# Loads on either of two queues, zeros first and a new written order: a recurrent attention with a two-layer network behind it, on one Trainium2 core

## The chip, the core and the metric

The kernel runs on one core of one Trainium2 chip. The core has a matrix engine (TensorE, PE in the profile; its weight loads are a row of their own, PEld), three elementwise engines (VectorE or DVE, ScalarE or ACT, GpSimd or POOL) and SyncE (SP), which here only issues transfers. Transfers run on 16 shared DMA engines. SyncE and GpSimd each issue into a queue of their own; each engine works through its instructions in the order in which they were written and waits on semaphores for what another engine or a transfer has to finish.

The metric is device time in microseconds (us) of an execution, the median of several. A profile is one further execution, recorded instruction by instruction; its span runs from the first instruction to the last.

## What is computed

```python
# q, k, v, alpha: (4, 8, 768, 48); w_in: (384, 2048); w_out: (2048, 384), all float32
state = zeros((B, H, D, D))
for t in range(S):
    state = alpha[:, :, t, :, None] * state + einsum('bhd,bhe->bhde', k[:, :, t], v[:, :, t])
    y[:, :, t] = einsum('bhd,bhde->bhe', q[:, :, t], state)
x = y.transpose(0, 2, 1, 3).reshape(B * S, H * D)      # 3072 tokens of 384
out = relu(x @ w_in) ** 2 @ w_out
```

## The kernel before

The 768 steps of each of the 4 sequences are cut into 3 blocks of 256 tokens, which gives 12 units, numbered 0 to 11: first block 0 of every sequence, then block 1, then block 2. Each unit goes through the same stages. In names below, g is the unit.

- *Loads.* Four transfers of 384 KB bring alpha, K, Q and V (`lda`g, `ldk`g, `ldq`g, `ldv`g, L545) into one of four RAW buffers. The two weights come in pieces, cast to bf16 on the way: `win0`, `win1`, `win2` (a quarter, a quarter and a half of w_in) and `wout0`, `wout1` (L513). A table AFTER holds some loads back until an earlier one has landed (`win2` until Q of unit 0, unit 2's loads until `win1`, `wout0` until `win2`, `wout1` until K of unit 2, unit 3's loads until `wout0`); from unit 5 on a load also waits for a step of the unit before.
- *Decays.* Logarithms of alpha (`ln`, from `pr`, the product of two tokens' alpha, for units 2 and up), summed over tokens by matmuls with triangular masks (`m1`), and exponentials of the sums (`ei`, `ea`, `es` on ScalarE); `bk`, `aq`, `lb` make the second token's terms.
- *Keys and queries.* K and Q are scaled (`ekm`, `eqm`) and transposed: on TensorE for units 0 to 2 (`tr`, L609 and L759, with copies `et` out of PSUM), by transposing DMAs from SyncE's queue (L747) for the others. V is cast to bf16 (`vc`, L726 and L727, L591 in unit 0).
- *Attention.* Scores (`p`, L925), a masked copy of them (`mk`, L936), states from K and V (`kv`, L796) with their updates (`sa`, `sc`, `sd`), and the output `y` of a unit (L817 to L864), copied to bf16 (`xe`) and transposed (`xt`; units 0 to 3 on TensorE, with a copy `xv`, the others by DMA, L977).
- *Dense layers.* The first layer has 8 groups of 6 matmuls a unit (`s1_g_u`, L1029), each ended by a maximum with 0 (`re`, on ScalarE L1037 or VectorE L1039); the squares (`sq`) are taken on VectorE (L1047), GpSimd (L1050) or ScalarE (L1051). The second layer has 8 groups of 4 matmuls (`s2_g_j_s`, L1070), copied out (`oe`) and stored (`out`). The last 128 tokens' are cut in two by columns (L997).

Hidden columns 0 to 3 of every 16 (in blocks of 128) need `win0`, 4 to 7 `win1`, the others `win2`; so groups 0 and 1 of a unit need `win0`, 2 and 3 `win1`, 4 to 7 `win2`. Second-layer quarters 0 and 1 need `wout0`, 2 and 3 `wout1`.

What decides the order is a table ORDERS: for each of the five engines the whole sequence of its steps, by name, found by a search ahead of time and written into the source. Steps without a name are numbered by creation (`#11` and `#12` fill two masks, `#21` and `#22` cut them, `#23` copies part of one on ScalarE, `#20` cuts an identity matrix, `#19` fills ZERO). A step stands in the list of the engine that does it, so the table also says which engine does a step that has a choice (`alts`). A planner (`Program.schedule`) runs the sequences against costs in nanoseconds; the kernel takes from it the times by which it leaves out waits that another wait implies. The method `fill` puts matmuls over ZERO into TensorE's idle time ahead of the first dense group, beginning when ZERO is filled by the plan; in ORDERS, ZERO's fill (`#19`) is the last step of VectorE, behind the last copy of the kernel, and no such matmul stands in the built kernel: TensorE's first instruction is that of L567 at 4.93 us.

The start of TensorE's list before, with what bears on the change: `m10_0 m11_0 tr00_0 tr10_0 tr01_0 tr11_0 kv0 p0_0 p1_0 m11 y0 tr0_1 xt0 tr1_1 p0_1 s1_0_2 s1_0_0 s1_0_1 kv1 s1_0_3 y1 s1_0_5 s1_0_4 s1_0_6`. (`m11` without an index behind it is unit 1's `m1`.)

Of the kernel before, what the change touches and what calls it, by code (L numbers as in the profile page):

```python
# [3 lines left out]
ALU = mybir.AluOpType  # L4
# [9 lines left out]
        table ln0_0 ln1_0 ei0_0 #23 ei1_0 ea0_0 ec0_0 ea1_0 vc0 et01_0 ec1_0 ln1 ei1 ea1 xe0 et0_1 ec1 re0_2 re0_0  # L14
        re0_1 sq0_3 re0_5 re0_4 ln2 re0_6 re0_7 es2 ei2 sq0_7 re1_2 ea2 re1_3 sq0_6 re1_5 et1_2 re1_6 sq1_7 sq1_6
        sq1_5 ec2 sq1_1 ln3 oe0_0 ei3 ea3 ec3 es3 vc3 oe1_0 lm4 ln4 ei4 ea4 ec4 oe0_1 es4 re2_0 re2_1 oe1_1 re2_3
        sq2_3 re2_4 ln5 lm5 ei5 ea5 ec5 xe3 re2_7 re2_6 sq2_6 es5 re3_0 re3_1 oe2_0 vc5 re3_3 lm6 xe4 ln6 re3_4 ei6
        oe2_1 re3_7 ea6 ec6 es6 oe3_0 re4_1 re4_0 re4_3 ln7 xe5 ei7 ea7 lm7 ec7 es7 sq4_5 re4_6 re4_7 re5_0 re5_1
# [8 lines left out]
        mk1_0 ekm1 eqm1 xv0 et1_1 sc0 mk1_1 mk0_1 sa1 #2 re0_3 sq0_1 xe1 pr2 xv1 sq0_5 sc1 re1_0 re1_1 bk2 ekm2 eqm2
        re1_4 et0_2 re1_7 mk1_2 mk0_2 sa2 pr3 sc2 bk3 eqm1_3 ekm3 aq3 eqm0_3 pr4 xe2 sa3 xv2 lb4 ekm4 eqm1_4 eqm0_4
        sc3 re2_2 mk1_3 mk0_3 re2_5 sq2_5 sa4 ekm5 xv3 sc4 lb5 eqm1_5 eqm0_5 mk1_4 mk0_4 re3_2 sq3_3 sa5 re3_5 sc5
        sq3_5 bk6 ekm6 re3_6 lb6 eqm1_6 eqm0_6 mk1_5 mk0_5 re4_2 sq4_1 sa6 re4_4 re4_5 sc6 lb7 oe3_1 ekm7 eqm1_7  # L30
        eqm0_7 mk1_6 mk0_6 sd6 re5_3 sa7 sc7 sq5_3 lb8 ekm8 oe4_1 eqm1_8 eqm0_8 mk1_7 mk0_7 sq5_7 sq6_1 re6_2 xe7
# [12 lines left out]
        s2_3_0_3 s1_4_1 s1_4_0 s2_3_1_0 s1_4_3 s2_3_1_1 s1_4_2 y5 s1_4_4 m1i7 s1_4_5 s2_3_1_2 s2_3_1_3 s1_4_7 p0_6
        s1_4_6 s2_4_0_0 s2_4_0_1 s1_5_0 s1_5_1 s2_4_0_2 s1_5_2 s1_5_3 y6 s2_4_0_3 s1_5_4 m1i8 s1_5_5 s2_4_1_0 s2_4_1_1
        s2_4_1_2 s2_4_1_3 s1_5_7 s1_5_6 s2_5_0_0 p0_7 s2_5_0_1 s1_6_0 s1_6_1 s2_5_0_2 s1_6_2 y7 s1_6_3 s2_5_0_3 s1_6_4
        s1_6_5 m1i9 s2_5_1_0 s2_5_1_1 s2_5_1_2 s1_6_7 s1_6_6 s2_5_1_3 p0_8 s1_7_1 s1_7_0 s2_6_0_0 s2_6_0_1 s1_7_3 y8
        s1_7_2 s2_6_0_2 s1_7_5 s2_6_0_3 s1_7_4 m1i10 p0_9 s2_6_1_0 s1_7_7 s2_6_1_1 s1_7_6 s2_6_1_2 s2_6_1_3 s1_8_1
        s1_8_0 s2_7_0_0 s1_8_3 s2_7_0_1 s1_8_2 y9 m1i11 s2_7_0_2 s1_8_4 s2_7_0_3 s1_8_5 s1_8_6 s2_7_1_0 s2_7_1_1
# [1109 lines left out]
```

## Time and profile before

| | |
|---|---|
| Median of 3 runs | 177.78 us (175.22, 177.78, 178.06) |
| Profiled execution, time | 173.93 us |
| Profiled execution, span | 172.2 us |
| Data moved | 33.37 MB in 71,559 packets, 67,568 of them under 512 bytes |
| GpSimd's queue | 8 loads of 384 KB and the 5 pieces of weight |
| SyncE's queue | 40 loads of 384 KB, 18 + 8 transposes, 14 stores |

The profile's first part gives the busy time of each engine and its share of the span. The windows give the same for stretches of the span, in the order PE, PEld, DVE, ACT, POOL, with the number of instructions in brackets, then the granted TensorE clock, the mean share of the DMA engines and GB/s. The chain of waits follows the work that ended last back through what released it. In a timeline each row is one instruction or a merged run of equal ones: start, length, engine, line, operation, output and input; what stands in square brackets is the idle time before it and what ended it. A share of the DMA engines can exceed 1 where packets overlap. Matmuls overlap too: the distance between starts tells their rate, not their length.

### The profile page before, as it was taken

The page shows a single profiled execution, that of the slowest core. Times are in us where ns is not written, and L with a number is a line of the kernel's source. Part 1 is how long each engine was busy: PE and PEld are TensorE (multiplying, and loading weights), DVE is VectorE, ACT ScalarE, POOL GpSimd, SP SyncE. Part 2 cuts the span into 40 slices and gives each one's busy share as a digit, 9 for nine tenths or more (in the row PEclk, how much of TensorE's full clock was granted, in tenths as well). Part 3 has the DMA queues.
Part 4 walks back from the last instruction along what each step waited for, and adds up shares of the span by engine and source line. Part 5 has one row for each costly group of instructions (what it writes and reads, how often), then busy time and mean ns, then how long its engine had stood idle before and what let it go on. Part 6 is the DMA issues. An engine that isn't in the chain of part 4 may idle for free.

```text
span 172.2 us, 5038 instructions
## 1 busy us (share of the span) xinstructions
PE 160.9 (93%) x2200; PEld 127.6 (74%) x2200; DVE 117.2 (68%) x186; ACT 104.5 (61%) x190; POOL 64.6 (37%) x65
## 2 busy tenths in 40 slices
PE   0696999999999999999999999999999999999994
PEld 0564799756788877887877887878777877687773
DVE  4478889768977787769566848799517709355241
ACT  2837478767677866466785578377668454152240
POOL 4947214910286554481640466001012122403700
PEclk9999999999999999999999999999999999999999
DMA  5999999999997999999999999999983672220012
GB/s 139 346 256 244 291 276 212 204 272 297 159 240 183 292 221 179 221 222 251 205 221 293 219 197 243 162 286 317 183 209 115 90 84 93 48 93 0 24 71 91
DMA packets 71559, 33.37 MB, mean 194 GB/s; under 512 B 67568, under 2 KB 68592, under 8 KB 71536
## 3 DMA queue, kind: packets, MB, share of 16 engines
q1 hardware_dynamic: 69024, 26.75, 70.4%
q0 software_dynamic: 2512, 6.29, 15.4%
q8 instruction: 17, 0.28, 0.7%
q14 instruction: 6, 0.05, 0.1%
HBM read 25.17 MB, written 4.72 MB: 174 GB/s over the span
## 4 chain that ended last, share of the span: by engine, by line
PE 90%; DVE 3%; ACT 2%; DMA 2%; issue 1%; DVEq 0%; ACTq 0%
PE psWH L1029 36%; PE psO L1070 33%; PE psX L925 3%; PE psZ L796 2%; PE psX L828 2%; DMA raw<-in_alpha_dram 2%; PE psX L817 2%; PE psWH L1070 2%; PE psX L997 2%; PE psZ L925 1%; PE psWH L669 1%; DVE pm L936 1%; PE psO L1029 1%; PE psX L864 1%; PE psX L971 1%
## 5 line engine op out<-in xcount | busy, mean ns | idle before, releaser
L1029 PE MATMUL psWH<-xt,win 128*128 128x256 bf16 x552 | 71.0, 274 | 0.2 <-ACT rr L1037 0.2
L1070 PE MATMUL psO<-wout,gt 128*128 128x384 bf16 x352 | 66.3, 326 | 0.0
L1029 PEld LDWEIGHTS psWH<-xt,win 128*128 128x128 bf16 x552 | 61.4, 129 | 5.3 <-DVE xt L983 0.6
L1070 PEld LDWEIGHTS psO<-wout,gt 128*128 128x128 bf16 x352 | 33.4, 98 | 17.5 <-DVE gt L1047 0.5
L1037 ACT ACTIVATE rr<-psWH 128x512 bf16<-128x512 f32 x58 | 33.9, 595 | 15.4 <-PE psWH L1029 14.5
L1050 POOL TENSOR_TENSOR gt<-rr 128x1024 bf16<-128x1024 bf16 (+1 forms) x17 | 28.0, 1654 | 37.4 <-ACT rr L1037 20.8
L1039 DVE TENSOR_SCALAR rr<-psWH 128x512 bf16<-128x512 f32 x34 | 23.4, 690 | 19.5 <-PE psWH L1029 19.0
L1051 ACT ACTIVATE gt<-rr 128x512 bf16<-128x512 bf16 (+1 forms) x26 | 21.1, 824 | 5.8 <-DVE rr L1039 5.8
L1077 ACT ACTIVATE osb<-psO 128x384 f32<-128x384 f32 x18 | 8.8, 490 | 17.0 <-PE psO L1070 16.8
L936 DVE TENSOR_TENSOR pm<-psZ,caus 128x1024 bf16<-128x1024 f32 x12 | 14.6, 1220 | 3.1 <-PE psZ L925 3.1
L726 POOL CAST vbf<-raw 128x768 bf16<-128x768 f32 x8 | 6.7, 832 | 24.6 <-DMA raw<-in_v_dram 24.6
L936 DVE TENSOR_TENSOR pm<-psX,caus 128x1024 bf16<-128x1024 f32 x12 | 14.6, 1216 | 0.5 <-PE psZ L925 0.5
L1047 DVE TENSOR_TENSOR gt<-rr 128x1024 bf16<-128x1024 bf16 (+1 forms) x17 | 10.6, 625 | 2.9 <-ACT rr L1037 2.4
L687 POOL TENSOR_TENSOR ek<-ek,raw 128x384 f32<-128x384 f32 x6 | 6.5, 1082 | 15.8 <-ACT ek L680 15.8
L731 DVE TENSOR_TENSOR qks<-raw,eq 128x384 bf16<-128x384 f32 x18 | 9.4, 553 | 2.6 <-DMA raw<-in_q_dram 1.8
L736 DVE TENSOR_TENSOR qks<-raw,ek 128x768 bf16<-128x768 f32 x11 | 10.5, 955 | 0.5 <-POOL ek L687 0.4
L704 DVE TENSOR_TENSOR la<-psWH,la 128x384 f32<-128x384 f32 x8 | 4.4, 553 | 7.9 <-ACT eq L682 6.5
L661 ACT ACTIVATE lab<-prd 128x384 bf16<-128x384 f32 x10 | 5.2, 522 | 4.1 <-POOL prd L660 2.4
L956 ACT ACTIVATE xbf<-psX 128x768 bf16<-128x768 f32 x7 | 5.7, 810 | 3.3 <-PE psX L817 3.0
L660 POOL TENSOR_TENSOR prd<-raw 128x384 f32<-128x384 f32 x5 | 5.2, 1040 | 4.9 <-DMA raw<-in_alpha_dram 4.9
L680 ACT ACTIVATE ek<-psWH 128x384 f32<-128x384 f32 x10 | 4.9, 490 | 3.0 <-PE psWH L672 2.2
L958 DVE CAST xbf<-psX 128x768 bf16<-128x768 f32 x5 | 4.8, 954 | 2.0 <-PE psX L817 1.3
(128 smaller groups left out, 183.7 us busy)
## 6 DMA issues: line engine op xcount, KB each, us to landing
out_dram<-osb SPq DMA_DIRECT2D x11, 384.0 KB, 4.0
raw<-in_alpha_dram SPq DMA_DIRECT2D x10, 384.0 KB, 4.5
raw<-in_k_dram SPq DMA_DIRECT2D x10, 384.0 KB, 4.6
raw<-in_q_dram SPq DMA_DIRECT2D x10, 384.0 KB, 4.8
raw<-in_v_dram SPq DMA_DIRECT2D x10, 384.0 KB, 4.9
wout<-in_moe_w_out_dram POOLq DMA_DIRECT2D x2, 768.0 KB, 8.4
raw<-in_alpha_dram POOLq DMA_DIRECT2D x2, 384.0 KB, 6.5
raw<-in_k_dram POOLq DMA_DIRECT2D x2, 384.0 KB, 7.2
```

Source lines behind the costliest of these rows:

```text
L731: add("dve", lambda e, j=j, dst=dst: e.tensor_tensor(dst, RAW[r][:, 2, :, j, :].rearrange("p (n x) d -> p n x d", x=2), EQ[la][:, j].rearr ...
L736: add("dve", lambda e, a=a, E=E: e.tensor_tensor(QKS[qs][:, a, :, :, 0:D], RAW[r][:, 1 + a].rearrange("p h j d -> p j h d"), E[la][:].rear ...
L925: ins = pe.matmul(psT[64 * c:64 * c + 64, rr_, o:o + 128], keys, mov)
L936: add("dve", lambda e, hf=hf, psT=psT: e.tensor_tensor(PM[pm][:, hf].rearrange("p r n j t -> p (r n) (j t)"), psT[:, :, :].rearrange("p r ...
L1029: ins = pe.matmul(psF[:, i * T:(i + 1) * T], WIN[:, kk, hidden(fj)], mov, start=(kk == 0), stop=(kk == KT - 1))
L1037: add("act", lambda e, psF=psF, rr=rr: e.activation(rr, psF, AF.Relu), act_ns(512), pu + 600, reads=[keyF], writes=[("rr", rb, half)], nam ...
L1039: alts={"dve": (lambda e, psF=psF, rr=rr: e.tensor_scalar(rr, psF, 0.0, None, ALU.max), dve_ns(512))})
L1047: add("dve", lambda e, dst=dst, sq=sq: e.tensor_tensor(dst, sq, sq, ALU.mult), 148 + k * 267, pu + 1200, reads=[("rr", rb, h) for h in ran ...
L1050: alts={"pool": (lambda e, dst=dst, sq=sq: e.tensor_tensor(dst, sq, sq, ALU.mult), 200 + k * 840), "act": (lambda e, dst=dst, sq=sq: e.act ...
L1051: "act": (lambda e, dst=dst, sq=sq: e.activation(dst, sq, AF.Square), act_ns(k * 512))})
L1070: ins = pe.matmul(psS, GT[gt][:, fj, j, :], WOUT[:, fj, :], start=(fj == 0), stop=(fj == FT - 1))
L1077: add("act", lambda e, j=j, psS=psS: e.activation(OSB[ob][:, j], psS, AF.Copy), act_ns(DM), ps_ + 700, reads=[keyS], writes=[("osb", ob, j ...
```

## The change

The five sequences are replaced by newly searched ones. With them:

- Loads of units 1 to 11 may stand in SyncE's list or in GpSimd's (EITHER, `alts`). Eight move to GpSimd: K of 3, V of 4, K of 5, V of 7, alpha and K of 9, alpha and V of 11. V of unit 1 moves from GpSimd to SyncE. Unit 2's K is issued ahead of its Q, unit 1's Q ahead of its K.
- ZERO's fill (`#19`) is VectorE's first step. The method `fill` is gone; 21 matmuls over zeros stand in TensorE's list by name, 16 of 512 columns and 5 of 256: seven ahead of the first `m1`, the others in between up to the first dense group.
- ScalarE's `#23` stands ahead of the first logarithm. V of unit 0 is cast on GpSimd. `s1_0_2`, the first dense group, stands ahead of `p0_1`, the scores of unit 1.
- Of the steps that have a choice, 104 change between the elementwise engines: 36 from VectorE to ScalarE, 34 from ScalarE to VectorE, 10 from GpSimd to VectorE, 9 from GpSimd to ScalarE, 8 from ScalarE to GpSimd, 7 from VectorE to GpSimd.
- The planner's costs change: how GpSimd and VectorE hold each other up, a slow TensorE before 9,000 ns, the cost of a change of matmul shape, and some fixed durations.

```diff
-        m10_0 m11_0 tr00_0 tr10_0 tr01_0 tr11_0 kv0 p0_0 p1_0 m11 y0 tr0_1 xt0 tr1_1 p0_1 s1_0_2 s1_0_0 s1_0_1 kv1
-        s1_0_3 y1 s1_0_5 s1_0_4 s1_0_6 xt1 s1_0_7 m1s2 m1i2 s1_1_0 s1_1_1 s1_1_2 s1_1_3 s1_1_4 s1_1_5 s1_1_6 tr0_2
-        tr1_2 s1_1_7 s2_0_0_0 p0_2 s2_0_1_0 s2_0_1_1 s2_0_0_1 kv2 s2_0_0_2 s2_0_0_3 s2_0_1_2 m1i3 s2_0_1_3 s2_1_0_0
...
+        fill512_0 fill512_1 fill512_2 fill512_3 fill512_4 fill512_5 fill256_6 m10_0 m11_0 fill512_7 tr00_0 fill512_8
+        fill512_9 fill512_10 tr10_0 tr01_0 tr11_0 kv0 p0_0 p1_0 fill512_11 fill256_12 m11 fill512_13 fill512_14
+        fill512_15 fill512_16 fill256_17 y0 tr0_1 fill512_18 fill256_19 xt0 tr1_1 fill256_20 s1_0_2 p0_1 s1_0_0 s1_0_1
+        kv1 s1_0_3 y1 s1_0_4 s1_0_6 xt1 s1_0_7 m1i2 s1_0_5 m1s2 s1_1_2 s1_1_1 s1_1_0 s1_1_5 tr0_2 s1_1_3 s1_1_4 tr1_2
+        s1_1_6 s2_0_0_0 p0_2 s2_0_0_1 s1_1_7 s2_0_0_2 s2_0_0_3 s2_0_1_0 kv2 s2_0_1_1 m1i3 s2_1_0_0 s2_1_0_1 s2_1_0_2
...
     "pool": """
-        #22 #15 #21 #14 #20 lda1 ldk1 ldq1 win1 win0 ldv1 win2 lda2 ldq2 ldk2 ldv2 vc1 wout0 wout1 aq2 sq1_3 sd1 sd0
-        vc2 sd2 bk4 sq2_1 pr5 vc4 sd3 bk5 sq2_7 sq3_1 sd4 pr6 sq3_7 sq3_6 vc6 sd5 pr7 sq4_3 bk7 vc7 pr8 sq5_1 bk8 vc8
-        pr9 sq6_3 bk9 sq6_6 sq6_5 vc10 bk11 vc11 sq9_3 sq9_7 sq10_1 sq10_6 sq11_1 sq11_3
+        #21 #22 #14 #15 lda1 #20 ldq1 ldk1 win1 vc0 win0 win2 lda2 ldk2 vc1 ldq2 sd0 ldv2 wout0 wout1 sq0_6 aq2 sq1_3
+        ldk3 vc2 sq1_7 ldv4 pr4 bk4 ldk5 sd3 pr5 sq2_3 bk5 sd4 vc5 pr6 sq3_3 bk6 vc6 sd5 sq4_3 ldv7 bk7 sq4_6 pr8
+        sq5_3 lda9 ldk9 vc8 bk9 sq6_3 sq6_6 sq6_5 lda11 sq7_7 pr11 sq8_3 ldv11 vc11 sq9_7 sq9_6 sq10_1 sq10_3
     """,
     "sp": """
-        lda0 ldk0 ldq0 ldv0 lda3 ldq3 ldk3 ldv3 lda4 ldk4 ldv4 ldq4 tr0_3 tr1_3 lda5 ldk5 tr0_4 tr1_4 out0_1 ldq5 ldv5
...
+        lda0 ldk0 ldq0 ldv0 ldv1 lda3 ldq3 ldv3 lda4 ldq4 ldk4 tr0_3 tr1_3 lda5 out0_1 tr0_4 tr1_4 ldq5 ldv5 out1_1
...
+    EITHER = tuple(range(1, G))
...
-            load_op[name] = add(ring, lambda e, dst=dst, src=src: e.dma_start(dst, src), cost, at,
-                writes=[key], name=f"ld{name}", dma=f"{nm}{r}{ring}", lag=1230 if ring == "sp" else 1180,
+            go = lambda e, dst=dst, src=src: e.dma_start(dst, src)
+            load_op[name] = add(ring, go, cost, at,
+                writes=[key], name=f"ld{name}", dma=f"{nm}{r}", lag=1230 if ring == "sp" else 1180,
+                alts={"sp": (go, 600), "pool": (go, 930)} if g in EITHER else None,
...
+    for name in ORDERS["pe"].split():
+        if name.startswith("fill"):
+            n = int(name[4:7])
+            add("pe", lambda pe, n=n: pe.matmul(psO[:, 0:n], ZERO[:, 0:128], ZERO[:, 0:n], skip_group_check=True),
+                216 if n == 512 else 109, 0, reads=[("zero",)], name=name)
     pr.schedule()
-    pr.fill(lambda n: lambda pe: pe.matmul(psO[:, 0:n], ZERO[:, 0:128], ZERO[:, 0:n], skip_group_check=True),
-            ((512, 216, 420), (256, 109, 250)), min(o.start for o in pr.order["pe"] if o.name.startswith("s1_")), zero, 4600)
```

More of the change, by code (lines that the diff above doesn't have):

```diff
@@ L13 @@
     "act": """
[L14 to L18, printed above, removed]
@@ L27 @@
[L27 to L31, printed above, removed]
@@ L44 @@
[L44 to L48, printed above, removed]
```

119 lines of the change are left out of this document (56 added, 63 removed).

## The prediction

> **What bounds the kernel now.** I read the page first, then the busy time by stage, then the chain of waits of the first 21 us, then the timelines of the queues that load. The span and the busy shares:
>
> ```profile
> span 172.2 us, 5038 instructions
> PE 160.9 (93%) x2200; PEld 127.6 (74%) x2200; DVE 117.2 (68%) x186; ACT 104.5 (61%) x190; POOL 64.6 (37%) x65
> ```
>
> The view of busy time by windows cuts the span in three (PE, PEld, DVE, ACT, POOL busy, clock, DMA share, GB/s):
>
> ```profile
> 1.00:18.20 17.20, 9.73 (x187) 7.50 (x188) 11.63 (x30) 9.73 (x18) 11.64 (x17) 1.00 1.06 259
> 18.20:170.00 151.80, 151.21 (x2018) 120.14 (x2014) 105.03 (x155) 94.60 (x172) 52.71 (x45) 1.00 0.86 189
> 170.00:172.20 2.20, 0.00 (x0) 0.00 (x0) 0.45 (x2) 0.00 (x0) 0.00 (x0) 1.00 0.28 89
> ```
>
> From 18.2 to 170 TensorE is idle for 0.6 us in all. A new order can win next to nothing there; it can only lose. What can be won lies ahead of 18.2, where TensorE is idle for 7.5 us. There the chain of waits reads (start, length):
>
> ```profile
> 6.36 0.30 ACT caus L485
> 9.26 1.03 PE psZ L609 x8
> 10.29 0.76 PE psWH L796 x16
> 11.04 0.60 PE psX L925 x16
> 12.81 1.23 DVE pm L936
> 16.40 0.56 DVE xt L983
> 16.96 0.61 DVE kqt L766
> 17.61 0.42 PE psX L925 x16
> 18.25 0.78 PE psO L1029 x6
> 20.34 0.45 PE psZ L796 x16
> ```
>
> L1029 at 18.25 is the first dense group; everything dense waits for it. Two things are to be seen. A mask for later use (6.36) stands between two exponentials that the chain needs. And the dense group stands behind the scores of unit 1 (17.61), which wait for a copy that it doesn't need: its own input is copied by 16.96.
>
> The early matmuls are also slow. TensorE's timeline shows the same work twice:
>
> ```profile
> 9.26 1.03 PE L609 MATMUL psZ<-ident,qks 128*128 128x128 bf16 x8 [0.42 <-DVE kqt L616]
> 11.98 0.45 PE L633 MATMUL psWH<-laf,linc 128*128 128x384 bf16 x1
> 12.26 0.33 PE L634 MATMUL psWH<-laf,linc 128*128 128x384 bf16 x1
> 12.42 0.33 PE L635 MATMUL psWH<-laf,linc 128*128 128x384 bf16 x1
> 14.99 0.62 PE L759 MATMUL psZ<-ident,qks 128*128 128x128 bf16 x8
> ```
>
> Eight transposes take 1.03 at 9.26 and 0.62 at 14.99; the 384-column matmuls follow each other after 0.28 at 11.98 and 0.16 at 12.26. So TensorE ran at about half rate until 12.2, though the page's clock row stands at 9 throughout and doesn't show it.
>
> The transfers set a second bound. GpSimd's and SyncE's timelines, with what ended each wait, the first uses on TensorE, and the DMA by stage:
>
> ```profile
> 4.56 1.09 POOL L545 DMA_DIRECT2D raw<-in_alpha_dram  x1 [0.35 <-DMA raw<-in_alpha_dram]
> 13.90 0.93 POOL L545 DMA_DIRECT2D raw<-in_alpha_dram  x1 [3.36 <-DMA win<-in_moe_w_in_dram]
> 17.63 0.82 POOL L726 CAST vbf<-raw 128x768 bf16<-128x768 f32 x1 [0.17 <-DMA raw<-in_v_dram]
> 21.44 0.71 POOL L513 DMA_DIRECT2D wout<-in_moe_w_out_dram  x1 [2.98 <-DMA win<-in_moe_w_in_dram]
> 25.69 0.58 POOL L513 DMA_DIRECT2D wout<-in_moe_w_out_dram  x1 [3.55 <-DMA raw<-in_k_dram]
> 22.30 0.87 PE L1029 MATMUL psO<-xt,win 128*128 128x256 bf16 x6
> 35.72 1.48 PE L1070 MATMUL psO<-wout,gt 128*128 128x384 bf16 x8
> 4.00:20.00 16.00, 11.54 (x203) 9.30 (x204) 11.30 (x18) 9.52 (x19) 10.57 (x13) 1.00 1.13 277
> 28.00:34.00 6.00, 6.00 (x86) 5.16 (x85) 4.90 (x7) 5.05 (x10) 4.53 (x4) 1.00 0.92 195
> wout<-in_moe_w_out_dram POOLq DMA_DIRECT2D x2, 768.0 KB, 8.4
> ```
>
> The last third of the first weight (win2) is there at 21.44 and first used at 22.30, 0.9 later. The second half of the other (wout1) is issued at 25.69, lands 8.4 later at 34.1 and is first used at 35.72, 1.6 later. The DMA share is over 1 up to 20 and 0.92 from 28 to 34: these landings go by bytes, and TensorE is only 0.9 and 1.6 us behind them.
>
> **The change, part by part.** The sum is made against the profiled execution, 173.93 (span 172.2 and 1.73 around it).
>
> *Start.* The mask goes ahead of the first logarithm, while ScalarE waits for data: -0.30. Zeros are filled first, and 21 matmuls over zeros (16 of 512 columns, 5 of 256) keep TensorE busy from about 1.3. If that brings full rate, the slow pieces of the chain shrink to their later sizes: transposes 1.03 to 0.62, states 0.76 to 0.45, scores 0.60 to 0.42, together -0.90. The price of the zeros: 512 columns are an estimate of 0.37 each at the slow spacing and 0.21 at the fast one; seven run before TensorE has anything to do, the other fourteen are 2.5 to 4.4 us in an idle time of some 3.5, so they could delay it by 1. V of unit 0 is cast on GpSimd instead of ScalarE: 4.56 + 1.09, a selection, two loads, a weight's issue and the cast end near 9.3, and the states are due at 10.29 - 0.30 - 0.41 = 9.6, so it costs nothing. Dense group 2 goes ahead of the scores of unit 1: 18.25 becomes 16.96 plus a little, -1.2. Together the first dense group starts near 15.8 instead of 18.2, -2.4.
>
> *What the transfers leave of it.* In the new order the first group that needs win2 comes after unit 1's output. The same work took 4.7 before (17.61 to 22.30); from 15.8 on that is 20.5, and the masks, whose scores now start a group later, make it some 21.0. win2 is there at about 21.4: -0.8 against 22.30. wout1 waits for K of unit 2, which moves from third to second of its unit, one issue of 0.89 earlier; I take wout1 0.7 earlier, at 33.4. The new order needs it sooner: it puts two second-layer groups and a state (1.4, as eight such matmuls at 35.72 take 1.48 with their tail, and 0.45 at 20.34; 1.9 in all) behind that point, which is 33.9 at the old pace. So 33.9 - 33.4 leaves -0.5. The ends: wout1 no earlier, +0.2; TensorE's own pace, -0.8. The zeros' possible 1 us is covered by the 1.9 that the transfers take back.
>
> V of unit 1 moves to SyncE's queue. The DMA queues differ in their packets (packets, MB, share of 16 engines):
>
> ```profile
> q1 hardware_dynamic: 69024, 26.75, 70.4%
> q0 software_dynamic: 2512, 6.29, 15.4%
> ```
>
> Share times span times 16 over the count gives 28 ns for a packet of SyncE's queue (q1) and 169 ns for one of GpSimd's (q0). If the engines serve the two in turn, V's 64 packets on each engine (1,024 runs of 384 bytes over 16) wait for one of GpSimd's each: 64 x 197 ns from about 7 ends near 20, where it was 17.6 (the cast at 17.63). Cast, state, output and the next dense group then follow near 23.1, 0.8 behind the old 22.30. That is the start's bad end, +0.8; bytes alone bring V no later than now, and I take that, since GpSimd itself stands waiting for win1 until 13.90 in that time and its queue runs thin.
>
> *The steady part.* Eight loads move from SyncE to GpSimd and one the other way:
>
> ```profile
> 34.00:132.00 98.00, 97.60 (x1388) 76.59 (x1386) 73.98 (x110) 67.75 (x126) 35.98 (x32) 1.00 1.05 225
> L545 POOL DMA_DIRECT2D raw<-in_k_dram x2 | 1.8, 890 | 0.0
> POOL vbf L726 <- DMA raw<-in_v_dram: 24.6, 6, 8.7
> POOL prd L660 <- DMA raw<-in_alpha_dram: 4.9, 5, 1.6
> ```
>
> Each holds GpSimd 0.89, net 6.2 us. GpSimd is busy 36 of the 98 us from 34 to 132, and that idle time hides them. SyncE's queue, with the transposes behind those loads, is relieved, but TensorE waits for none of them now. ScalarE's, VectorE's and GpSimd's elementwise steps are dealt out anew, with about the same sums. The ends are -0.6 (the idle time above) and +6.2 (each load felt whole); I take +0.1, beside the lower end, because of the 62 idle us.
>
> [...]
>
> *The end.* VectorE's 0.45 after 170 holds the zeros' fill, which moves to the start; the last stores run beside it: 0. The planner's changed costs emit no instruction: 0.
>
> Sum: 173.93 - 0.5 + 0.1 = 173.5, for an execution like the profiled one.
>
> **From there to the median.** The runs shown go from 175.22 to 178.06 with the median at 177.78, so 3.85 over the profiled execution. Something early can differ that much. From 18.2 on TensorE never rests, so each us at half rate costs 0.5. If half rate lasted beyond 12.2, unit 0's output, the transposes, the second scores would cost an estimated 1.0 more (by 0.41 for eight transposes, 0.18 for scores), and 2.85 more would take 5.7 us of dense work at half rate, until near 25. I take this for the likelier cause, since the trace shows TensorE leaving half rate only after 3 us of nearly unbroken work (9.26 to 12.2), and the next unbroken stretch begins at 17.6. The new kernel is busy with zeros from 1.3 and nearly without a gap from 4.9, so each execution should come to full rate before 12, and the median falls to the sum: 173.5.
>
> [...]
>
> **The rivals.**
>
> *The spread stays.* If the 3.85 come from transfers (the DMA share is over 1 up to 20), or the zeros don't bring full rate sooner, the new kernel keeps that distance: 177.78 - 0.4 = 177.4, no change. For it: the early landings go by bytes. Against: the waits for them are short in TensorE's time, 0.9 and 1.6 us of margin. A part of the spread removed gives 174.3 to 177.
>
> *GpSimd's queue becomes the bound.* It works in order, and a load at its head waits for its buffer and for the load before it. The two rows of waits show it standing for V up to 8.7 at once and 4.1 on average (24.6 by 6), for alpha 1.0 (4.9 by 5). Today a cast or product follows such a wait; in the new order squares for the second layer follow moved loads too, and TensorE takes a late square as a stall. If each of the seven loads is felt with its 0.89 and 0.3 to 1.0 of wait, the sum grows by 8 to 13: 182 to 187, I name 182.5, slower. It decides from 1.1 us per load over the likeliest case, or 0.6 if the spread stays. Against: 62 us of idle time.
>
> **The numbers.** A measurement of this kernel tells about 2% from no change: 174.2 and 181.3 are the bounds. The forecast has 0.46, nearly all of it under 174.2; the spread staying, wholly or partly, 0.34; GpSimd's queue as the bound 0.20. So faster 0.46, within 2% 0.34, slower 0.20. The likeliest case alone reaches from 172.6 (-0.8 and -0.6 in place of -0.5 and +0.1) to 174.7 (+0.8 in place of -0.5, about 1.2 higher). The range goes on to the spread's 177.4 and one us more for the start's bad end on top of it: 172.0 to 178.5, which leaves the slower case out.
>
> **What would show it.** Right: the first dense group (L1029) near 16, ahead of the scores; matmuls of 384 columns 0.16 apart before 12; the wait of the first wout1 group short, or none; TensorE idle under 1 us from 34 to 170; runs close to each other. Wrong: transposes at 9 still near 1.03; V of unit 1 landing after 19; stalls in the middle whose releaser is a square or cast on GpSimd, or a moved load; or a spread as wide as before.

## The result, and the profile after

| | time (us) | ratio to before, 95% interval |
|---|---|---|
| Before, in the same measurement | 176.5 (174.72 to 178.06) | |
| After | 184.18 (182.49 to 184.99) | 1.051 [1.0405, 1.0616] |
| After, a second measurement | 181.44 (178.27 to 183.05) | 1.0278 [1.0131, 1.0426] |
| After, a third, on another chip | 179.33 (177.88 to 182.09, and one of 420.26) | 1.0229 [1.0174, 1.0284] |

The change makes the kernel slower, by 2 to 5 points, where 173.5 and a gain had been forecast. A ratio compares only fast executions, those within 1.5% of the fastest of their kernel, while medians and ranges take in all. (The execution of 420.26 us comes back in the last section.) The profiled execution of after took 184.99, the longest of the first measurement's four. Its page begins with the span and the busy shares, and the fourth part gives the shares of the chain that ended last; the last row is that part before:

```profile
span 183.2 us, 5075 instructions
...
PE 164.7 (90%) x2219; PEld 127.2 (69%) x2221; DVE 120.0 (65%) x187; ACT 107.8 (59%) x193; POOL 65.8 (36%) x68
...
PE 50%; DMA 38%; DVE 5%; POOL 3%; issue 2%; ACT 2%; POOLq 0%; DVEq 0%
...
PE 90%; DVE 3%; ACT 2%; DMA 2%; issue 1%; DVEq 0%; ACTq 0%
```

No engine's busy time grew by more than 3.8 us, the span by 11.0, and transfers hold 38% of the chain where they held 2%. The view of waits, TensorE alone, from 18 us on (total, times, longest), says where TensorE stood:

```profile
PE psWH L1009 <- DMA xt<-xbf: 3.8, 3, 1.5
PE psWH L649 <- ACT lab L641: 2.8, 2, 1.9
PE psX L905 <- DMA kqt<-qks: 1.9, 1, 1.9
PE psO L1050 <- DVE osb L1059: 1.6, 1, 1.6
PE psO L1050 <- DMA wout<-in_moe_w_out_dram: 0.5, 1, 0.5
PE psX L837 <- DVE smd L874: 0.3, 1, 0.3
```

10.9 us in all, against 0.4 in the same view before; 10.5 of the 11.0 are these waits. The dense layer (L1009) waits for transposing DMAs of the output; the first sums of decays (L649) for a cast of ScalarE whose input alpha came late; the scores (L905) for transposed keys; a second-layer group (L1050) for a copy by VectorE that stands in the list behind two products of Q, which wait for a load.

The worst place is unit 4's two transposes. SyncE's timeline, the issues between 49 and 50 with their microseconds to landing, and the windows (PE, PEld, DVE, ACT, POOL, clock, DMA share, GB/s):

```profile
49.35 3.80 SPq L727 DMA_TRANSPOSE kqt<-qks  x2
59.79 0.37 SPq L523 DMA_DIRECT2D raw<-in_q_dram  x1
```

```profile
raw<-in_k_dram POOLq DMA_DIRECT2D x1, 384.0 KB, 10.0
kqt<-qks SPq DMA_TRANSPOSE x1, 10.4
```

```profile
53.00:55.00 2.00, 2.00 (x69) 1.88 (x69) 1.25 (x3) 1.75 (x4) 1.60 (x1) 1.00 1.33 117
55.00:57.00 2.00, 2.00 (x20) 1.57 (x18) 1.74 (x4) 1.83 (x5) 1.68 (x2) 1.00 1.09 84
57.00:59.00 2.00, 1.67 (x15) 1.31 (x12) 0.00 (x0) 1.61 (x4) 0.11 (x1) 1.00 0.98 91
```

K of unit 5, now on GpSimd's queue, is in flight beside them; all three take some 10 us (the second transpose 9.8), and the DMA engines, busy throughout, move 84 to 117 GB/s. Q of unit 5, behind the transposes on SyncE's queue, is issued only at 59.79. That made the moved loads my first suspect. The second profile of the same kernel (178.27) doesn't show it:

```profile
span 176.5 us, 5075 instructions
```

```profile
PE psWH L1009 <- DMA xt<-xbf: 2.7, 2, 1.6
PE psWH L649 <- ACT lab L641: 1.3, 1, 1.3
PE psWH L1009 <- ACT osb L1057: 0.6, 1, 0.6
PE psX L837 <- DVE smd L874: 0.3, 1, 0.3
```

Unit 4's transposes land in 6.3 and 5.5 there; 4.9 us of waits are left, 4.5 over before's 0.4, and the span is 4.3 longer. So the loss is TensorE's waiting, some 4.5 us of it in a good execution and 10.5 in a bad one. Most of the 4.9 belongs to three output transposes, and unit 5's shows how. Its issue, its microseconds to landing and its first use, before and in the second profile:

```profile
76.08 2.02 SPq L977 DMA_TRANSPOSE xt<-xbf  x1
xt<-xbf SPq DMA_TRANSPOSE x1, 4.5
81.68 1.47 PE L1029 MATMUL psWH<-xt,win 128*128 128x256 bf16 x12
...
76.97 1.94 SPq L957 DMA_TRANSPOSE xt<-xbf  x1
xt<-xbf SPq DMA_TRANSPOSE x1, 6.3
83.40 1.47 PE L1009 MATMUL psWH<-xt,win 128*128 128x256 bf16 x12 [1.62 <-DMA xt<-xbf]
```

Before, it landed at 80.56 and was used 1.12 later. The output transposes of units 4 to 8 landed 0.47 to 1.87 ahead of their first use there, those of units 9 to 11 2.85 to 3.98 ahead. In the changed order TensorE comes for those of units 5, 6 and 8 4.5 to 4.8 after their issue, where it came 5.1 to 6.3 after, and they take 5.0 to 6.3, where they took 4.5. It stands 1.62, 0.64 and 1.12 for them. (The view puts the 0.64 down to a copy; that transpose landed 0.14 ahead of the group's start, as the other two did.)

At the start, the first dense group:

```profile
17.26 0.84 PE L1009 MATMUL psO<-xt,win 128*128 128x256 bf16 x6
```

It came at 18.19 before, and at 16.74 in the second profile.

### The profile page after: what moved, and what is told of

The parts are those of the page before. It is cut to its first block, busy times and chain, and to the rows that moved or that the text cites. A ratio compares the mean times of both kernels' runs of the same rounds, so it can differ in the third digit from the quotient of the medians.

```text
span 183.2 us, 5075 instructions
## 1 busy us (share of the span) xinstructions
PE 164.7 (90%) x2219; PEld 127.2 (69%) x2221; DVE 120.0 (65%) x187; ACT 107.8 (59%) x193; POOL 65.8 (36%) x68
## 4 chain that ended last, share of the span: by engine, by line
PE 50%; DMA 38%; DVE 5%; POOL 3%; issue 2%; ACT 2%; POOLq 0%; DVEq 0%
PE psO L1050 22%; PE psWH L1009 18%; DMA kqt<-qks 9%; DMA xt<-xbf 6%; DMA wout<-in_moe_w_out_dram 5%; DMA raw<-in_q_dram 5%; DMA raw<-in_k_dram 4%; DMA win<-in_moe_w_in_dram 4%; DMA raw<-in_alpha_dram 3%; POOL raw L523 2%; PE psX L808 2%; PE psWH L1050 2%; PE psZ L776 2%; PE psX L977 1%; PE psX L797 1%
## 5 line engine op out<-in xcount | busy, mean ns | idle before, releaser
L1009 PE MATMUL psWH<-xt,win 128*128 128x256 bf16 x552 | 70.1, 273 | 3.9 <-DMA xt<-xbf 3.8
L1050 PE MATMUL psO<-wout,gt 128*128 128x384 bf16 x352 | 66.7, 326 | 2.1 <-DVE osb L1059 1.6
L1009 PEld LDWEIGHTS psWH<-xt,win 128*128 128x128 bf16 x552 | 61.7, 129 | 9.7 <-ACT osb L1057 3.0
L1017 ACT ACTIVATE rr<-psWH 128x512 bf16<-128x512 f32 x67 | 39.3, 595 | 39.0 <-PE psWH L1009 38.3
L1050 PEld LDWEIGHTS psO<-wout,gt 128*128 128x128 bf16 x352 | 32.8, 98 | 19.8 <-DVE osb L1059 1.9
L1019 DVE TENSOR_SCALAR rr<-psWH 128x512 bf16<-128x512 f32 x25 | 17.2, 687 | 8.0 <-PE psWH L1009 7.7
L1031 ACT ACTIVATE gt<-rr 128x1024 bf16<-128x1024 bf16 (+1 forms) x24 | 21.1, 893 | 1.3 <-DVE rr L1019 1.1
L1027 DVE TENSOR_TENSOR gt<-rr 128x1024 bf16<-128x1024 bf16 (+1 forms) x19 | 13.1, 693 | 6.2 <-ACT rr L1017 6.2
L716 DVE TENSOR_TENSOR qks<-raw,ek 128x768 bf16<-128x768 f32 x11 | 10.5, 954 | 5.1 <-DMA raw<-in_k_dram 5.0
L706 POOL CAST vbf<-raw 128x768 bf16<-128x768 f32 x6 | 5.0, 830 | 18.9 <-DMA raw<-in_v_dram 18.9
L1057 ACT ACTIVATE osb<-psO 128x384 f32<-128x384 f32 x13 | 6.4, 491 | 6.4 <-PE psO L1050 6.3
L523 POOL DMA_DIRECT2D raw<-in_alpha_dram x4 | 3.8, 959 | 16.6 <-ACT rr L1017 8.0
L871 DVE TENSOR_TENSOR smd<-psZ,sbd 128x384 bf16<-128x384 f32 x8 | 4.4, 554 | 7.3 <-PE psX L797 7.3
L1059 DVE COPY osb<-psO 128x384 f32<-128x384 f32 x9 | 5.0, 557 | 6.1 <-PE psO L1050 6.1
L938 DVE CAST xbf<-psX 128x768 bf16<-128x768 f32 x7 | 6.7, 953 | 3.3 <-PE psX L797 2.2
```

The costliest lines, as they stand in the source:

```text
L523: go = lambda e, dst=dst, src=src: e.dma_start(dst, src)
L716: add("dve", lambda e, a=a, E=E: e.tensor_tensor(QKS[qs][:, a, :, :, 0:D], RAW[r][:, 1 + a].rearrange("p h j d -> p j h d"), E[la][:].rear ...
L938: alts={"dve": (lambda e: e.tensor_copy(XBF[x2][:], psX[:, :, 0:HD]), dve_ns(2 * HD))})
L1009: ins = pe.matmul(psF[:, i * T:(i + 1) * T], WIN[:, kk, hidden(fj)], mov, start=(kk == 0), stop=(kk == KT - 1))
L1017: add("act", lambda e, psF=psF, rr=rr: e.activation(rr, psF, AF.Relu), act_ns(512), pu + 600, reads=[keyF], writes=[("rr", rb, half)], nam ...
L1019: alts={"dve": (lambda e, psF=psF, rr=rr: e.tensor_scalar(rr, psF, 0.0, None, ALU.max), dve_ns(512))})
```

## The experiments

In the names of experiments, "back" is the changed program with the eight moved loads on SyncE's queue again. Ratios are to the kernel before on the same chip, whose median lay between 174.79 and 176.13 there. The theories have letters; A to D stand in the first expectations, E to I come with the results. One thing holds for all runs called "the kernel before with" something, but the one with thin stores alone: they are the changed program with the old lists put in, so the planner's changed costs, and with them the choice of the waits that are left out, are in them too. The three with least else changed (one load moved, and zeros at the start) come out at 1.0038 to 1.0051, so these costs are worth about half a point at most, unless those edits won back what the costs lost.

### Is it the moved loads?

```diff
 pool: -ldk3 -ldv4 -ldk5 -ldv7 -lda9 -ldk9 -lda11 -ldv11
 sp:   ... ldq3 +ldk3 ldv3 lda4 ldq4 ldk4 +ldv4 tr0_3 tr1_3 lda5 +ldk5 out0_1 tr0_4 ... xt5 +ldv7 ...
```

> The changed kernel with all eight loads issued by SyncE again, everything else as changed. Theory A (loads from GpSimd's queue and SyncE's transposing DMAs in flight together hold each other up): the transposes of unit 4, 10.4 us in the changed kernel, land in 4 to 6.5; the three stalls of TensorE that follow them (1.9, 1.6, 1.9 us) and the 1.5 us before unit 7's dense groups go; time 176 to 178.5 against 184.2. Theory B (the new dealing of the elementwise steps is what is late, wherever the loads are issued): 182.5 to 185.

180.67 us, 1.0313 [1.0241, 1.0386]; stalls of 7.6 us. Unit 4's transposes took 5.9 and 4.0 and TensorE didn't wait for them, as theory A had it, but the time lies between both theories' ranges: most of the waiting has another cause. Next, the one suspect alone (K of unit 5 back on SyncE's queue), and the same load alone moved in the kernel before:

> The changed kernel with one load, K of unit 5, issued by SyncE again. Theory A: unit 4's transposes land in 4 to 6.5 us instead of 10.4, and the stalls of 1.9, 1.6 and 1.9 us go with this one load: 178 to 180.5. Theory B: within 1 us of the changed kernel, 183 to 185.

181.68 us, 1.0269 [1.0159, 1.0379], between the theories again and with a wide spread (178.01 to 185.97).

> The kernel before with one load moved, K of unit 5 to GpSimd's queue behind unit 4's second-token product, so that it is issued about when unit 4's transposes are. Theory A: that load and the two transposes land after 8 to 10.5 us instead of 4.6 and 4.0 to 6.2, TensorE waits for unit 4's scores, and the time grows by 2 to 5 us over the kernel before. Theory B: the load lands in 5 to 7 us and the time stays within 1 us.

177.1 us, 1.0051 [1.0018, 1.0083]; the load was issued at 46.68, ahead of the transposes, and landed in 5.4, they in 6.9 and 5.5: theory B's numbers. So it was put later, behind them:

```diff
 pool: ... bk4 sq2_1 +ldk5 pr5 ...
```

> The kernel before with K of unit 5 moved to GpSimd's queue as in the last such run, but three steps later in its list, so that it is issued at about 49.6 us, after the two transposes of unit 4 (from 47.4 us) and not before them as then (46.7 us). Theory A (a load on GpSimd's queue that is issued while SyncE's transposes are in flight holds these up): the transposes land 9 to 10 us after their issue instead of 6.2 and 6.9, the load in some 10, and the ratio is 1.01 to 1.02. Rival (the 10 us in the changed kernel came from something else that lay there, the store issued at 48.1 or unit 4's other loads): 6 to 7 us, ratio 1.005 or less.

175.91 us, 1.0038 [0.9987, 1.0089]. The load was issued at 50.74, two us behind the transposes (48.70), as in the changed kernel's bad place; it landed in 6.0 and they in 5.4 and 6.2, near the rival's numbers. All eight in the kernel before:

```diff
 pool: ... sd1 +ldk3 ... vc2 +ldv4 ... bk4 +ldk5 ... sq4_3 +ldv7 ... sq5_1 +lda9 bk8 +ldk9 ... sq6_5 +lda11 ... bk11 +ldv11 ...
```

> The kernel before with the eight loads moved to GpSimd's queue at about the times at which they were issued, all other orders as before. The forecast's step on the steady part (eight loads cost 0.89 us each on an engine that idles): 1.00 to 1.005. Theory A (each such load that is in flight beside SyncE's transposes holds them up): 1.015 to 1.03, with transposes or loads that land 8 to 10 us after their issue.

179.29 us, 1.024 [1.0157, 1.0324]. The ratio is theory A's, but not its long landings: behind 30 us none took 8, and unit 4's transposes took 7.0 and 6.6. Its two large stalls, 1.91 and 1.57 us, come by GpSimd. The first: VectorE's two products of Q before, then in this run, with GpSimd's square and the second of the two masked copies behind the products, for which TensorE waited until 63.53:

```profile
57.88 1.03 DVE L731 TENSOR_TENSOR qks<-raw,eq 128x384 bf16<-128x384 f32 x2 [0.87 <-DMA raw<-in_q_dram]
...
58.48 2.73 DVE L715 TENSOR_TENSOR qks<-raw,eq 128x384 bf16<-128x384 f32 x2 [1.43 <-DMA raw<-in_q_dram]
58.88 1.91 POOL L1034 TENSOR_TENSOR gt<-rr 128x1024 bf16<-128x1024 bf16 x1 [2.13 <-ACT rr L1021]
62.27 1.21 DVE L920 TENSOR_TENSOR pm<-psX,caus 128x1024 bf16<-128x1024 f32 x1
```

Q came 0.6 later, so the second product started at 58.96, just behind the start of GpSimd's square, and ended at 61.21, 0.4 behind its end: it took 2.25 instead of 0.55. Before, the second was under way when the square began (58.84) and ended at 58.91. The second stall comes from where I had put a load in GpSimd's list (start, length, idle time before and its end):

```profile
92.58 0.93 POOL L527 DMA_DIRECT2D raw<-in_alpha_dram  x1 [3.35 <-ACT rr L1021]
93.53 1.02 POOL L671 TENSOR_TENSOR ek<-ek,raw 128x384 f32<-128x384 f32 x1
```

The load stands at the head of the list for 3.35 us, and the product behind it, which VectorE needs, starts at 93.53, where the kernel before had it at 88.34. In the changed kernel that product (`bk8`) is VectorE's, so nothing of the kind follows this load there.

Then the direct comparison, both kernels on one chip:

> The changed kernel, measured beside the next one on one chip. Theory A (the moved loads cost about 2 of the 5 points): 1.04 to 1.05, 1 to 2 points above the next kernel. Theory I (the loss is the new orders' alone; where the loads are issued decides only which transfer is late): within half a point of the next kernel, both at 1.025 to 1.045.

> The changed program with the eight loads on SyncE's queue, measured beside the kernel above. Theory A: 1.02 to 1.03. Theory I: the same as the kernel above to half a point.

After 179.33 us, 1.0229 [1.0174, 1.0284]; loads back 179.86 us, 1.0306 [1.0241, 1.037]. The moved loads cost nothing in the new orders on this chip; the 0.8 of a point by which the kernel with them is ahead isn't clear of the intervals. Theory A falls as the cause of the loss here. Theory I holds in kind; its half a point was missed by a little. The first measurement's 1.051 was never set beside the loads back on one chip, so what its 2 to 3 points more are isn't shown, and the 10 us landing remains a fact of one profile.

### Is it the new start?

The zeros and ZERO's early fill, put into the kernel before:

> The kernel before with ZERO filled first and the 21 matmuls over zeros in TensorE's list, nothing else moved. Theory C (the spread of the kernel before comes from when TensorE leaves half rate): full rate by the first sums at 5 us, runs within 1.2 us of each other, median 173 to 174.5. Theory D (the spread comes from transfers): full rate by 5 us as well, but runs that spread by 2 to 4 us as before and a median of 175.5 to 177.5.

177.5 us, 1.0043 [0.9993, 1.0094], 174.49 to 182.43. Full rate by 5 us, which both theories had taken for granted, wasn't there in the profiled execution: its 192-column matmuls at 4.9 follow each other after 0.14 to 0.16, much as before (0.13 to 0.16), where the changed kernel's first profile has 0.08. The spread didn't shrink, so theory C falls, and 0.75 us gained at unit 2's state (34.52 for 35.27) were gone at the end.

### Is it single places in the new orders?

The program with the loads back waits in the dense layer for three output transposes, once for a copy and once for a cast. Where such a transposing DMA stands in SyncE's list (its rows in the loads-back program, and the transfer's landing):

```profile
76.41 1.17 SPq L528 DMA_DIRECT2D raw<-in_k_dram  x1
78.40 0.37 SPq L528 DMA_DIRECT2D raw<-in_q_dram  x1
78.81 1.45 SPq L962 DMA_TRANSPOSE xt<-xbf  x1
```

```profile
xt<-xbf SPq DMA_TRANSPOSE x1, 5.1
```

Its input was ready at 77.23 (76.29 and 0.94 for the cast). It was issued 1.58 later, behind Q, and landed 5.1 after that.

```diff
 sp: ... +xt5 ldk7 ldq7 -xt5 ... +xt6 ldk8 ldq8 -xt6 ... +xt8 ldv10 ldq10 out5_1 -xt8 ...
```

> The changed program with all eight loads on SyncE's queue, and in SyncE's list the transposes of the output of units 5, 6 and 8 put ahead of the two loads, of K and Q of a later unit (8: of V, Q and a store), that stood before them. Theory E (what is left of the loss after the loads are back is cover that the new order took from three kinds of transfers and steps: the output's transposes are issued behind loads, land 5 to 6 us later instead of 3.5 to 4.5, and the dense layer waits for them): the three stalls of 1.36, 1.35 and 0.97 us go, the span falls from 179.2 by 3 to 3.7 us, the ratio from 1.031 to about 1.01. Theory F (the landing is slow because the cast ahead of it now lies on VectorE, or because of whatever else is in flight, not because of the place in the list): the transposes land as late as before and the ratio stays at 1.03.

182.56 us, 1.0422 [1.0328, 1.0517]. The three transposes landed in 2.8 each where they had taken 5.1, 6.1 and 5.7, and the waits for them are gone. Other waits took their place, 7.8 us in all for 7.6:

```profile
PE psWH L1014 <- DVE rr L1024: 4.5, 3, 2.5
PE psX L910 <- DMA kqt<-qks: 1.9, 1, 1.9
PE psWH L654 <- ACT lab L646: 1.0, 2, 0.7
```

VectorE's timeline shows what its maximum (L1024), for which TensorE now waits, had to stand behind:

```profile
84.54 0.96 DVE L721 TENSOR_TENSOR qks<-raw,ek 128x768 bf16<-128x768 f32 x1 [3.16 <-DMA raw<-in_k_dram]
85.42 0.68 DVE L1024 TENSOR_SCALAR rr<-psWH 128x512 bf16<-128x512 f32 x1
...
98.93 0.56 DVE L716 TENSOR_TENSOR qks<-raw,eq 128x384 bf16<-128x384 f32 x1 [4.42 <-DMA raw<-in_q_dram]
99.41 0.68 DVE L1024 TENSOR_SCALAR rr<-psWH 128x512 bf16<-128x512 f32 x1
```

The loads that were passed came late, and everything behind them on VectorE with them. Theory E is right about why a transpose lands late, and wrong in taking that for the cost: what one transfer gains the next one loses. The 2.9 us by which the span grew, 182.1 for 179.2, are another matter. Unit 6's scores already start 2.1 later (82.09 for 79.98), ahead of the first moved transpose's use: TensorE had stood 1.92 for unit 4's keys, which the move doesn't touch, and its granted clock had fallen to half behind that wait (0.50 from 60 to 62). It fell once more behind the wait of 2.46 that came with the move (0.52 from 102 to 104; last section).

```diff
 dve: ... sq2_6 +oe2_0 eqm0_5 eqm1_5 -oe2_0 ...
 pe:  ... s1_3_4 -m1i6 s2_2_1_2 y4 s2_2_1_3 +m1i6 ...
```

> The changed program with all eight loads on SyncE's queue, and two steps moved: the eviction of unit 2's first dense output ahead of unit 5's two Q products on VectorE (which wait for a load), and unit 6's first cumulative matmul two matmul groups and one output step later on TensorE. Theory E: the stalls of 1.2 us (dense output on its eviction) and 0.8 us (that matmul on ScalarE's cast) go, about 2 us of the span, the ratio from 1.031 to about 1.02. Rival (the wait only moves on, since the loads of units 5 and 6 are late whatever waits for them): the stalls come back within 3 us at the Q products, the scores of unit 5 or the dense layer, and the ratio stays at 1.03.

181.6 us, 1.0375 [1.0297, 1.0453]: both stalls went. A wait of 1.97 came at unit 4's scores, with a fall of the clock behind it (0.50 from 60 to 62), but that is ahead of both moved steps; behind them the dense layer waited 1.07 for ScalarE. The rival's ratio came, then, without its mechanism being shown. From unit 6's scores to the end this execution takes 97.0 us, and two profiles of the same program without the two moves (loads back, on two chips) take 99.3 and 97.3: one profile can't settle 2 us here.

> Both of these edits together in the changed program with its loads on SyncE's queue. Theory E: 5 to 5.7 us off the span of 179.2, ratio 1.00, and TensorE's idle time after 34 us under 2.5 us. The rival of a loss that moves on: 1.015 to 1.03.

183.45 us, 1.0476 [1.0394, 1.0559], above both ranges. 8.0 us of waits are left, the longest, 2.55, for VectorE's maximum, again with a fall of the clock behind it (0.55 from 100 to 102). Places cured singly gave nothing back.

### Is it SyncE's list, or the compute lists?

> The changed program with its loads on SyncE's queue, and with SyncE's whole list taken from the kernel before (V of unit 1 is the one load that has no place there and goes behind unit 0's); the lists of the four compute engines are the changed ones. Theory H (the order on SyncE's queue is at fault: transfers stand there in an order that lands the wrong ones late): the span falls to 172 to 175 us, ratio 1.00 to 1.01. Theory G (the DMA engines are a second bound, busy for 97 to 117% of every 10 us from 10 to 120 us in the kernel before, so that no order lands the loads sooner, and the changed compute orders ask for some units about three matmul groups earlier than they can come): stalls of 5 to 8 us stay, at other places, ratio 1.03 to 1.04.

181.5 us, 1.0215 [1.0096, 1.0334], between the two; the stalls stay (6.9 us), as theory G said, at other places: one transpose now takes 6.8 and holds the dense layer for 2.48.

> The kernel before with SyncE's list in the changed order (all loads on SyncE's queue, but V of unit 1, which stays on GpSimd's as before). Theory H: 1.02 to 1.03. Theory G, with the compute orders at fault: 1.00 to 1.01.

178.62 us, 1.0159 [1.0055, 1.0262]. Both halves cost: SyncE's new list alone 1.6 points with the old compute lists, and the new compute lists some 2 points even with SyncE's old list. Both intervals exclude no change and are about 2 points wide. Neither H nor G as put holds the whole.

### Is it the time of the transfers?

The stores of units 0 to 10 cut to an eighth:

```diff
-    e.dma_start(dst, OSB[ob][:].rearrange("p j n -> p (j n)"))
+    e.dma_start(dst[:, :96], OSB[ob][:].rearrange("p j n -> p (j n)")[:, :96])
```

> The changed kernel whole, but for the stores of units 0 to 10, which write an eighth of their bytes (96 of 768 numbers of a row): some 11% less to move, all orders and queues as they are, the output incomplete. Theory G (what the changed orders lose is lost to transfers that the DMA engines have no time for): the stalls at transposes and loads shrink to 1 to 4 us and the ratio to 1.00 to 1.02. Rival (the stalls come from the order of waits among engines whatever the DMA engines have to move): 1.04 to 1.05 as in the whole kernel.

176.3 us, 1.0022 [0.9971, 1.0073]: theory G's ratio. The whole kernel wasn't run on this chip, but this interval lies below all three of the whole kernel. What is left of the stalls isn't known: the profiled execution took 182.65, far from that median, and stood 7.9 us. The control:

> The kernel before with the stores of units 0 to 10 cut to an eighth of their bytes, as in the changed kernel's thin run. Theory G (in the old order the transfers just keep up, and TensorE, idle for 0.6 us, is the bound): 0.990 to 1.000, so that the 5 points which the thin stores gave the changed kernel are its own. Rival (the thin stores help any order alike): 0.95 to 0.97.

174.86 us, 0.9992 [0.9952, 1.0032]: the old order gains nothing from 11% less to move, so what the thin stores gave the changed kernel, 2 to 5 points by the measurement, is its own.

> The changed program with all loads on SyncE's queue (ratio 1.031 in full) and the thin stores. Theory G: 0.99 to 1.005, stalls of TensorE after 18 us of 2 us in all or less. Rival (the new compute orders wait in their own lists): 1.015 to 1.03.

177.47 us, 1.0134 [1.0033, 1.0235], between the two: by the middle values more than half of 1.0306 is gone; 4.6 us of stalls are left.

```profile
PE psWH L1014 <- DMA xt<-xbf: 2.6, 3, 1.1
PE psWH L654 <- ACT lab L646: 1.4, 2, 0.8
PE psX L910 <- DMA kqt<-qks: 0.6, 1, 0.6
```

> The kernel before with the eight loads on GpSimd's queue (ratio 1.024 in full) and the thin stores. Theory G (all of the loss is transfers' time): 0.99 to 1.005. Rival (a part is GpSimd's own list: an issue of 0.93 us ahead of a product that VectorE waits for, as at 92.6 us in the full run, where TensorE then stood 1.57 us): 1.008 to 1.015.

180.48 us, 1.0302 [1.0186, 1.0417]: no help here, and above both ranges. The load at the head of GpSimd's list held it for 4.32 us at the same place, and TensorE stood 2.21 for what followed, with a fall of the clock behind it (0.52 from 98 to 100): the rival's mechanism, dearer than it said.

> The changed kernel as it is, profiled a second time. Theory A in its strong form: the transposes of unit 4 take 9 to 10 us again beside the load of K of unit 5 on GpSimd's queue. Weak form (any transfers that meet there; the 10 us was the worst of several arrivals): 6 to 9 us. The ratio is 1.04 to 1.06 in both.

1.0278 [1.0131, 1.0426], 6.3 and 5.5 us for the transposes: the strong form falls, and the weak one's 6 to 9 and its ratio are hardly reached either.

**What is shown, and what stays open.** The loss is TensorE waiting at some five places of the new lists. The same lists with fewer bytes to store lose less, down to 1.002 in the whole change, while the old order gains nothing from them. With the margins of the output transposes above (0.47 to 1.87 us before, none at three places after) that says: the old order keeps a small slack ahead of each transfer that TensorE needs, and the new one doesn't. The loads' queue isn't the cause where it was tested.

Open are the 1.3 points that remain with thin stores and the loads back, why one execution let three transfers take 10 us, and whether fewer bytes help by the engines' time or by freeing SyncE's queue sooner. A rival for part of the loss wasn't tested: VectorE's products of two SBUF tiles, held while GpSimd works, as in the stall of 1.91. In the profile before, none is lengthened; in the changed kernel's first profile seven, squares among them, took 3.9 us more in all than the shortest of their kind. How much TensorE waited for that isn't known. TensorE's list alone wasn't tried in the other program: with the other lists as they are, each order waits for what the other puts later.

## The prediction, point by point

- *"A new order can win next to nothing there; it can only lose."* Right, and then not priced.
- **The failed step is the steady part: +0.1.** Its reason was that SyncE's queue "is relieved, but TensorE waits for none of them now", with the elementwise steps dealt out anew "with about the same sums". That TensorE waits for no transfer is a property of the old order, not of the transfers, and it hung on margins of 0.47 to 1.87 us at a DMA share of 1.05. In the stretch that the term was read from, 34 to 132, TensorE is idle for 4.85 us in the second profile and 9.78 in the first, where it was 0.40: +4.5 and +9.4. The term's bad end of +6.2 was made for another thing, each load felt whole on GpSimd. That GpSimd's idle time hides the loads' issues was right in the new orders: 1.0229 with them, 1.0306 without. In the old order it wasn't, 1.024, by where the loads stood.
- *The start, -0.5.* The first dense group came at 17.26 and 16.74, not 15.8 (15.96 in one experiment). `wout1` was issued at 25.77 in the first profile, no earlier than before, which is the sum's bad end of +0.2, and at 24.01 in the second, 1.7 earlier, more than the 0.7 forecast. The span without the waits is 176.5 - 4.5 = 172.0 in the second profile, 0.2 under before's: next to nothing of the 0.5 was left at the end. The cast of V of unit 0 on GpSimd wasn't quite free: in the first profile unit 0's states stood 0.36 for it, until 9.44.
- *From the profile to the median.* Half rate at the start was taken for the cause of the spread, and this step failed as well. The zeros do what they were meant to: in TensorE's timelines the first matmuls at full rate start between 4.83 and 10.89 us in nine profiles with zeros, and between 11.83 and 18.81 in six without. (At 5.07 in the first profile, whose 192-column matmuls were 0.08 apart; only at 10.04 in the second, where four transposes took 0.40, after 0.61 at 6.99.) But an execution of the old order with half rate until 17.7 (thin stores; eight transposes at 16.94 took 1.06 there, 0.61 at 16.20 in the profile before) has a span of 173.2, 1.0 over 172.2. So half rate, held that long, explains about 1 of the 3.85. With zeros in the old order the spread was wider, and the changed kernel's own runs go from 178.27 to 183.05 on one chip. In the five later measurements before's median was 174.79 to 176.13, so the 177.78 that the step set out from was itself high.
- *V of unit 1.* The bad end wasn't reached: its cast came at 18.12 (17.63 before) in the first profile, right behind another issue and without a wait of its own, and at 16.39 in the second.
- *GpSimd's queue becomes the bound, 182.5, with 0.20.* The time came near (179.33 to 184.18), by luck: no late square on GpSimd holds TensorE in either profile. A load that holds GpSimd's list up was seen only where I moved the loads into the old order (3.35 us, TensorE 1.57).
- *"The spread stays", 177.4.* The spread did stay, but the time is above that too: this rival also put nothing on the steady part.
- *What would show it wrong* named stalls in the middle with a square, a cast or a moved load as releaser. Stalls there are, far over the 1 us, but at their head stands a kind that wasn't named, the output's transposes.
- *A load's issue on GpSimd, 0.89.* This number held: after's loads took 0.88 to 1.06 to issue there, the four of alpha 0.96 in the mean (below). What the forecast had nothing for is VectorE held by GpSimd's own work, as in the stall of 1.91 above.

```profile
L523 POOL DMA_DIRECT2D raw<-in_alpha_dram x4 | 3.8, 959 | 16.6 <-ACT rr L1017 8.0
```

## What to carry to other kernels

Where the engine that bounds the kernel hardly waits (0.4 us here) and the DMA engines are full too (a share of 1.05), that absence of waits can belong to the order, as it did here. A reordering is then to be priced by the slack of each transfer (landing to first use), not by busy sums: it was 0.5 to 1.9 us at the output's transposes, against a forecast of 0.1. When a stall at one transfer is cured by moving it ahead of others on the same queue, look at once for who needs those others. And before a moved instruction is blamed, the whole change and the change without it should run side by side on one chip: here the same kernel stood at 1.051, 1.028 and 1.023 in three measurements.

## What the runs showed of the hardware that was not expected

*Some stalls cost more than their length.* After a wait of 1.92 us (the experiment with the transposes first) TensorE's timeline shows twelve dense matmuls in 2.65 us, which take 1.47 elsewhere, and the windows show the granted clock, the third number from the right:

```profile
58.83 0.42 PE L910 MATMUL psX<-kqt 64*64 64x128 bf16 x16 [1.92 <-DMA kqt<-qks]
59.07 0.39 PE L910 MATMUL psZ<-kqt 64*64 64x128 bf16 x16
59.40 1.37 PE L1055 MATMUL psO<-wout,gt 128*128 128x384 bf16 x4
60.56 2.65 PE L1014 MATMUL psWH<-xt,win 128*128 128x256 bf16 x12
...
105.06 1.47 PE L1014 MATMUL psWH<-xt,win 128*128 128x256 bf16 x12
```

```profile
58.00:60.00 2.00, 1.17 (x35) 0.82 (x36) 0.24 (x1) 1.09 (x2) 0.00 (x0) 0.88 0.87 190
60.00:62.00 2.00, 2.00 (x10) 1.29 (x9) 1.98 (x4) 0.00 (x0) 0.00 (x0) 0.50 1.00 300
62.00:64.00 2.00, 2.00 (x14) 1.48 (x12) 1.62 (x2) 1.19 (x2) 0.82 (x1) 0.76 1.22 304
```

At half clock for 0.48 + 2.0 + 0.96 = 3.4 us, which is 1.7 us of work lost on top of the 1.92. The windows give the same fall, 3.40 to 3.44 us at half clock, behind waits of 1.97, 1.99, 2.21, 2.46 and 2.55 in five profiles. There is none behind one of 2.48 with SyncE's old list (granted clock 1.00, twelve dense matmuls in 1.47), nor behind one of 1.91 with all eight loads moved (1.00), one of 1.9 with K of unit 5 back (1.0 over the whole span) and two of 1.91 in after's first profile (twelve dense matmuls in 1.47 soon after one of them, four of the second layer in 0.81 after the other). So the length of a wait alone doesn't tell whether the clock falls; what does isn't shown.

*VectorE was held by GpSimd.* Products of two SBUF tiles that started while GpSimd was at a square or another elementwise step ended some 0.4 us after that one's end: 2.25 us instead of 0.55 above, and in after's first profile 1.10 at 26.77, 0.85 at 79.26, 0.99 at 112.32 and 0.89 at 130.84. In the run with all loads moved, a Q that landed 0.6 later was enough to meet it.

*A load at the head of GpSimd's list* held the list for 3.35 and 4.32 us (above).

*Transfers of two queues at once* took 10.0 and 10.4 us at 84 to 117 GB/s with the engines fully busy (a share of 0.98 to 1.33), in one profile of the changed kernel, and 6.0 (the load), 6.3 and 5.5 in the other.

*One execution of 420.26 us*: TensorE was busy for 414.2 of 418.5, the first dense layer's matmuls took 536 ns in the mean instead of 273, and of its 1.9 us of waits none was for a transfer. Its cause isn't known.
